# A Winograd-style convolution with batch norm and SiLU: new order of the start-up, and two weight sums on another engine

## The chip, the cores and the metric

The kernel runs on one core of a Trainium2 chip. The metric is device time in microseconds, as the median of several executions; smaller is better. A core has a matrix engine (TensorE, PE in the profile; its weight loads are PEld), a vector engine (VectorE, DVE), an activation engine (ScalarE, ACT), a general engine (GpSimd, POOL) and an engine that here only issues transfers (SyncE, SP). Each engine works through its own list of instructions in the order in which the program issues them; semaphores hold an instruction back until what it reads is there.

## The reference

`x` is bf16 of shape (2, 2048, 1024), `w` is (3, 1024, 1024), and `mean`, `var`, `g`, `b` have 1024 entries each.

```python
def reference(x, w, mean, var, g, b):
    xp = jnp.pad(x, ((0, 0), (1, 1), (0, 0)))
    y = sum(jnp.einsum('bsc,cd->bsd', xp[:, k:k + S, :], w[k]) for k in range(3))
    inv_std = 1.0 / jnp.sqrt(var + 1e-5)
    y = (y - mean) * (g * inv_std) + b
    return _silu(y)
```

So it is a convolution over the sequence with three taps, from 1024 to 1024 channels, then a per-channel scale and shift, then SiLU.

## The kernel before

**The algorithm.** The three-tap convolution is done as F(6, 3): six outputs from eight inputs with eight products instead of eighteen. A sequence of 2048 gives 342 tiles of six outputs. Three steps follow one another.

1. *Input transform* (`transform`, matmuls of L216). A window of up to 128 rows of `x` (21 tiles of six rows, plus two) is the stationary operand, and a small matrix `Rm` of 8 x 21 columns is the moving one. One matmul for each of eight channel blocks turns the window and applies the 8 x 8 transform at once. ScalarE (L230) or Vector (L232) evicts the result from PSUM into `T_sb`, whichever has less in a running count called `load`. There are 17 windows for each of the two batches.
2. *Weight transform.* The output channels are cut into eight chunks of 128. For a chunk the raw taps w0, w1, w2 (tile `wch`) give six transformed taps (tile `uch`, two buffers), in three pairs: a sum of the outer taps, `e` (names e1, e2, eh, fp32), then `e + odd` and `e - odd`, where for pairs 1 and 2 some taps are scaled first (`w0x`, `w1x`, `w2x`). Sums and taps are GpSimd's (L160 to L162); the scalings are ScalarE's (L148), for chunk 0 and part of chunk 1 GpSimd's (L146). Products 0 and 7 use raw taps.
3. *Products and inverse transform* (`unit`). A unit is one chunk and one batch, written (chunk, batch): 16 in all, in the order (0,0), (0,1), (1,0), ... Each has eight products of eight matmuls with 342 columns (L241), in the order 1, 3, 2, 4, 5, 7, 6, 0, into four banks A, B, C, G of PSUM. ScalarE copies partial results (`m1`, `m3`, `s1`, `s2`, `m5`, L280), and Vector combines them to six outputs `y` (L273, L305), the last of which, `y[0]`, needs product 0. ScalarE's SiLU (L317) is issued later, inside the next unit, from the list `late`; a transposing transfer and stores through SyncE bring the unit out.

**The order of the work.** The schedule is the program's order, written by hand. The start transforms batch 0. Inside that loop stand the loads of chunk 0 (L88), the parameter loads and, behind window 5, chunk 0's weight transform on GpSimd. Just before the last window `turn_params` transposes the parameters on PE (L182) and Vector copies them (L183); `make_params` then works out scale and shift on GpSimd. Next comes batch 1's loop: three groups of transforms per window, and between them the matmuls of unit (0,0), which here begins with product 7, in portions given by `want`, so that 52 of its 64 matmuls are spread over 51 groups. The remaining units follow one another.

**Where the weights of later chunks stand.** Ahead of each unit (dc, 1) the program issues the weight transform of chunk dc + 1 on GpSimd and ScalarE, then the unit itself. GpSimd has nothing else to do and runs ahead of PE as far as its buffers and inputs allow.

**Loads.** All x windows and weights go through SyncE's queue in the order of issue; the x windows of 256 KB have rows of 2 KB, chunk loads (256 KB for one tap) have rows of 256 bytes. Ten window buffers are in use. The first window has a buffer of its own, `xw0`, whose row 0 is zeroed. The matrix `Rm` is built from an iota (`val`, GpSimd), a comparison (`E`, Vector) and 25 multiply-adds on Vector (L116) for rows 1 to 6, and by eight selects on GpSimd (L128) for rows 0 and 7.

Of the kernel before, what the change touches and what calls it, by code (L numbers as in the profile page):

```python
# [30 lines left out]
NJ = 8  # L31
# [4 lines left out]
def kernel(  # L36
# [52 lines left out]

    open_weights(0)  # L90

    dummy = consts.tile([P, 2], FP32, name="dummy")
    nc.vector.memset(dummy, 0.0)
    nc.scalar.activation(dummy[:, 1:2], dummy[:, 0:1], ACT.Silu)


    xw0 = consts.tile([P, C], BF16, name="xw0")
    nc.gpsimd.memset(xw0[0:1, :], 0.0)
    Rm = consts.tile([P, NJ, WT], BF16, name="Rm")
    val = consts.tile([P, NJ, WT], I32, name="val")  # L100
    nc.gpsimd.iota(val, pattern=[[-1, NJ], [-M_OUT, WT]], base=0, channel_multiplier=1)
    E = consts.tile([P, NJ, WT], FP32, name="E")
    nc.vector.memset(Rm, 0.0)
    nc.vector.tensor_single_scalar(E, val, 0.0, op=ALU.is_equal)
    for k in range(NJ):
        j = 1
        while j < 7:
            v = BT[j][k]
            if v == 0:
                j += 1  # L110
                continue
            j1 = j
            while j1 + 1 < 7 and BT[j1 + 1][k] == v:
                j1 += 1
            nj = j1 - j + 1
            nc.vector.scalar_tensor_tensor(  # L116
                out=Rm[:, j:j1 + 1, :],
                in0=E[:, k:k + 1, :].to_broadcast([P, nj, WT]) if nj > 1 else E[:, k:k + 1, :],
                scalar=float(v),
                in1=Rm[:, j:j1 + 1, :],  # L120
                op0=ALU.mult,
                op1=ALU.add,
            )
            j = j1 + 1
    for j in (0, 7):
        for k in range(NJ):
            if BT[j][k] != 0:
# [9 lines left out]
    ident = consts.tile([P, P], BF16, name="ident")  # L137
    make_identity(nc, ident)
    yTs = [consts.tile([P, M_OUT, NP], BF16, name=f"yT{i}") for i in range(2)]

    def scale_weights(dc, taps=(2, 1, 0), on_gpsimd=False):
        for k in taps:
# [7 lines left out]
    def open_chunk(dc):  # L150
        wts[dc] = upool.tile([P, 6, CT, P], BF16, name="uch")

    def pair_weights(dc, n):

        w0, w1, w2 = raw[dc]
        e = wtmp.tile([P, CT, P], FP32, name=("e1", "e2", "eh")[n])
        a = wx[dc, 0] if n == 2 else w0
        c = wx[dc, 2] if n == 1 else w2
        odd = wx[dc, 1] if n else w1
        nc.gpsimd.tensor_tensor(e, a, c, op=ALU.add)  # L160
        nc.gpsimd.tensor_tensor(wts[dc][:, 2 * n], e, odd, op=ALU.add)  # L161
        nc.gpsimd.tensor_tensor(wts[dc][:, 2 * n + 1], e, odd, op=ALU.subtract)  # L162

    T_sb = [tpool.tile([P, CT, NJ, NTB], BF16, name=f"T_sb{bi}") for bi in range(B)]
    load = {"act": 0.0, "dve": 1.0}
    EVAC = {"act": (0.17, 0.14), "dve": (0.12, 0.17)}

    prm = consts.tile([4 * DC, P], BF16, name="prm")
    prmT = consts.tile([P, 4, DC], FP32, name="prmT")
    sk = consts.tile([P, DC], FP32, name="sk")  # L170
    beta = consts.tile([P, DC], FP32, name="beta")
    mhalf = consts.tile([P, DC], FP32, name="mhalf")
    rstd = consts.tile([P, DC], FP32, name="rstd")
    sc = consts.tile([P, DC], FP32, name="sc")

    def load_params():
        for q, ap in enumerate((var, g, mean, b)):
            nc.gpsimd.dma_start(out=prm[q * DC:(q + 1) * DC, :], in_=ap.rearrange("(dc p) -> dc p", p=P))

    def turn_params(bk):  # L180
        pv = ps_all[:, bk * 512:bk * 512 + 2 * DC].bitcast(BF16)
        nc.tensor.transpose(pv, prm, ident[0:4 * DC, 0:4 * DC])  # L182
        nc.vector.tensor_copy(prmT.rearrange("p q d -> p (q d)"), pv)  # L183

    def make_params():
        nc.gpsimd.memset(mhalf, -0.5)
        nc.gpsimd.tensor_scalar(rstd, prmT[:, 0, :], 1e-5, 1.0, op0=ALU.add, op1=ALU.mult)
        nc.gpsimd.tensor_tensor(rstd, rstd, mhalf, op=ALU.pow)
        nc.gpsimd.tensor_tensor(sc, prmT[:, 1, :], rstd, op=ALU.mult)
        nc.gpsimd.tensor_tensor(beta, prmT[:, 2, :], sc, op=ALU.mult)  # L190
        nc.gpsimd.tensor_tensor(beta, prmT[:, 3, :], beta, op=ALU.subtract)
        nc.gpsimd.tensor_scalar(sk, sc, C1, 0.0, op0=ALU.mult, op1=ALU.add)

    epool = ctx.enter_context(tc.tile_pool(name="epool", bufs=1))

    def load_window(xpool, bi, wi):
        ntile = min(WT, NTB - WT * wi)
# [53 lines left out]
    def unit(dc, bi, c0, c1, banks, yT, late, pace=(1, 0, 1, 1, 0), seven_first=False):  # L251

        nn = c1 - c0  # L260
        A, B_, C_, G = [ps_all[:, k * 512:k * 512 + nn] for k in banks]
        bA, bB, bC, bG = banks
        pace = list(pace)

        def et(name):
            return epool.tile([P, NTB], FP32, name=name)[:, 0:nn]

        m1, m3, m5, s1, s2, d1 = (et(n) for n in ("m1", "m3", "m5", "s1", "s2", "d1"))
        y_all = epool.tile([P, M_OUT, NTB], FP32, name="y")[:, :, 0:nn]
        y = [y_all[:, i] for i in range(M_OUT)]  # L270

        def stt(o, i0, s, i1, op1=ALU.add):
            nc.vector.scalar_tensor_tensor(out=o, in0=i0, scalar=s, in1=i1, op0=ALU.mult, op1=op1)  # L273
            load["dve"] += 0.0013 * nn

        def copy_out(dst, src):
            for _ in range(pace.pop(0)):
                if late:
                    late.pop(0)()
            nc.scalar.copy(dst, src)  # L280
            load["act"] += 0.0013 * nn

        if seven_first:
            yield from mms(bG, 7, dc, bi, c0, c1, True)
        yield from mms(bA, 1, dc, bi, c0, c1, True)
        copy_out(m1, A)
        yield from mms(bB, 3, dc, bi, c0, c1, True)
        copy_out(m3, B_)
        yield from mms(bA, 2, dc, bi, c0, c1, False)
        copy_out(s1, A)  # L290
        stt(d1, m1, 2.0, A, op1=ALU.subtract)
        yield from mms(bB, 4, dc, bi, c0, c1, False)
        copy_out(s2, B_)
        for i in (2, 4):
            stt(y[i], B_, ALPHA * 2.0 ** i, s1)
        stt(B_, m3, 2.0, B_, op1=ALU.subtract)
        yield from mms(bC, 5, dc, bi, c0, c1, True)
        copy_out(m5, C_)
        while late:
            late.pop(0)()  # L300
        for i in (1, 3, 5):
            stt(y[i], B_, ALPHA * 2.0 ** i, d1)
        if not seven_first:
            yield from mms(bG, 7, dc, bi, c0, c1, True)
        nc.vector.tensor_tensor(y[5], G, y[5], op=ALU.add)  # L305
        yield from mms(bC, 6, dc, bi, c0, c1, False)
        for i in (2, 4):
            stt(y[i], C_, BETA * 0.5 ** i, y[i])
        stt(G, m5, 2.0, C_, op1=ALU.subtract)
        yield from mms(bA, 0, dc, bi, c0, c1, False)  # L310
        for i in (1, 3, 5):
            stt(y[i], G, BETA * 0.5 ** i, y[i])
        stt(y[0], s2, ALPHA, A)
        stt(y[0], C_, BETA, y[0])

        def silu(i0, i1):
            nc.scalar.activation(  # L317
                yT[:, i0:i1:2, c0:c1],
                y_all[:, i0:i1:2],
                ACT.Silu,  # L320
                bias=beta[:, dc:dc + 1],
                scale=sk[:, dc:dc + 1],
            )

        late.extend(lambda i=i: silu(*i) for i in ((2, 5), (1, 6), (0, 1)))
# [10 lines left out]
    with tc.tile_pool(name="xwin", bufs=10) as xpool:  # L336
        for wi in range(NWIN):
            window = load_window(xpool, 0, wi)
            if wi == 1:
                load_chunk(0, 0)  # L340
                load_chunk(0, 2)
                load_params()
            if wi == 2:
                load_chunk(0, 1)
            for h in range(2):
                transform(0, wi, window, 4 * h, 4, (2 * wi + h) % 4 * 2, 2)
            if wi == 5:
                open_chunk(0)
                for n, taps in ((0, ()), (1, (2, 1)), (2, (0,))):
                    scale_weights(0, taps, on_gpsimd=True)  # L350
                    pair_weights(0, n)
            if wi == NWIN - 2:
                turn_params((2 * wi + 2) % 4 * 2)
        make_params()
        for yT in yTs:
            nc.gpsimd.memset(yT[:, :, NTB:NP], 0.0)

        first = unit(0, 0, 0, NTB, (0, 1, 2, 3), yTs[0], late, seven_first=True)
        load["act"] = load["dve"] = 0.0
        gi, done = 0, 0  # L360
        for wi in range(NWIN):
            window = load_window(xpool, 1, wi)
            if wi == 6:
                for k in (0, 2, 1):
                    load_chunk(1, k)
            for ct0, n in ((0, 3), (3, 3), (6, 2)):
                transform(1, wi, window, ct0, n, 4 + gi % 4, 3)
                gi += 1
                want = 52 * gi // (3 * NWIN)
                run(first, want - done)  # L370
                done = want
        load_weights(1)
# [42 lines left out]
    for ui, (dc, bi) in enumerate(units[1:-1], 1):  # L415
        yT = yTs[ui % 2]
        half = 4 * (ui % 2)
        if bi == 1 and dc + 1 < DC:
            open_chunk(dc + 1)
            pair_weights(dc + 1, 0)  # L420
            if dc == 0:
                scale_weights(1, (2,), on_gpsimd=True)
                scale_weights(1, (1, 0))
            else:
                scale_weights(dc + 1)
            for n in (1, 2):
                pair_weights(dc + 1, n)
        run(unit(dc, bi, 0, NTB, (half, half + 1, half + 2, half + 3), yT, late))
        if ui < len(units) - 2:
            late.append(lambda dc=dc, bi=bi, yT=yT: finish(dc, bi, yT))  # L430
# [89 lines left out]
```

## Time and profile before

| | |
|---|---|
| time, three executions | 195.18, 195.74 (median), 196.20 us |
| profiled execution | 196.92 us, of which the span of instructions is 195.1 us |
| PE busy | 177.8 us (91%) |
| POOL busy | 164.7 us (84%) |
| DVE busy | 149.4 us (77%) |
| ACT busy | 124.2 us (64%) |
| mean granted clock of TensorE | 0.979 |
| first transform, first product | 5.40 us, 22.66 us |
| moved by DMA | 31.72 MB, mean 163 GB/s |

The profile is that of one execution. Times in it are counted from the first instruction. A line of a timeline gives start, duration, engine, source line and operation, output and inputs with their shapes, and in brackets the idle time before it and what ended that. A merged line (x40) stands for instructions that followed each other without a pause. The table by stages gives each engine's busy time in a stretch of time, then the granted clock, the share of the DMA engines and the rate in GB/s.

### The profile page before, as it was taken

Reading aid. Unit: us, or ns where it says so; the run is one execution under the profiler, and the core shown is the slowest. Engines: PE = TensorE matmul, PEld = TensorE weight load, DVE = VectorE, ACT = ScalarE, POOL = GpSimd, SP = SyncE. Lnnn points to the kernel's source line nnn. Section 1 sums busy time; section 2 is a strip of 40 time slices with the busy share of each in tenths; the row PEclk is TensorE's granted clock in tenths of the full one; section 3 lists DMA queues with packets and bytes.
Section 4 is the critical chain, followed back from the end, with each engine's and each line's share of the span. In section 5 each row is a group of like instructions: output and inputs, shape, how many; then the busy total and the mean of one; then the engine's idle time right before and its main releaser. Section 6 shows DMA issues by size and latency. Waiting matters only on the chain.

```text
span 195.1 us, 3898 instructions
## 1 busy us (share of the span) xinstructions
PE 177.8 (91%) x1397; PEld 126.7 (65%) x1397; DVE 149.4 (77%) x345; ACT 124.2 (64%) x206; POOL 164.7 (84%) x105
## 2 busy tenths in 40 slices
PE   0779799989999999999999999999999999999840
PEld 0668588856666666666666666666666666679830
DVE  6369668996878696969696969686877878697880
ACT  3479558878378827873786287548736872827930
POOL 7899999999999999999999999999999999800000
PEclk9999879999999999999999999999999999999995
DMA  4999999900607487999292989774755657397505
GB/s 135 277 392 344 332 257 371 284 15 2 116 5 137 96 159 182 276 166 200 39 211 41 198 229 257 142 157 92 139 112 116 129 105 152 76 174 157 115 5 108
DMA packets 86823, 31.72 MB, mean 163 GB/s; under 512 B 73428, under 2 KB 82644, under 8 KB 86804
## 3 DMA queue, kind: packets, MB, share of 16 engines
q1 hardware_dynamic: 86637, 31.46, 69.8%
q8 instruction: 11, 0.18, 0.3%
q14 instruction: 8, 0.07, 0.1%
q0 software_dynamic: 128, 0.01, 0.0%
q10 hardware_dynamic: 39, 0.01, 0.0%
HBM read 14.82 MB, written 8.39 MB: 119 GB/s over the span
## 4 chain that ended last, share of the span: by engine, by line
PE 84%; DVE 7%; DMA 3%; SPq 2%; ACT 1%; issue 1%; DVEq 0%; ACTq 0%
PE ps_all L241 76%; PE ps_all L216 7%; DVE T_sb L232 4%; DMA xw<-in_x_dram 3%; DVE y L273 1%; SPq L206 1%; SPq L88 1%; PE ps_all L446 1%; DVE o_end L478 1%; DVE o_end L486 0%; ACT m L280 0%; ACT yT L317 0%; SPq L203 0%; SPq L202 0%; DVE ps_all L273 0%
## 5 line engine op out<-in xcount | busy, mean ns | idle before, releaser
L241 PE MATMUL ps_all<-T_sb,uch 128*128 128x342 bf16 (+2 forms) x816 | 123.9, 299 | 1.8 <-ACT m L280 1.8
L241 PEld LDWEIGHTS <-uch 128*128 128x128 bf16 x816 | 76.7, 97 | 34.5 <-issue 1.3
L317 ACT ACTIVATE yT<-y,beta,sk 128x684 bf16<-128x684 f32 (+8 forms) x51 | 47.1, 925 | 29.9 <-DVE y L273 29.8
L273 DVE SCALAR_TENSOR_TENSOR y<-ps_all,y 128x342 f32<-128x342 f32 (+2 forms) x102 | 45.4, 487 | 1.3
L241 PE MATMUL ps_all<-T_sb,wch 128*128 128x342 bf16 (+2 forms) x272 | 44.7, 303 | 0.1
L216 PE MATMUL ps_all<-Rm,xw 128*128 128x168 bf16 (+1 forms) x272 | 31.8, 248 | 8.5 <-DVE Rm L116 5.4
L280 ACT COPY m<-ps_all 128x342 f32<-128x342 f32 (+2 forms) x51 | 21.7, 427 | 20.6 <-PE ps_all L241 19.6
L230 ACT CAST T_sb<-ps_all 128x672 bf16<-128x672 f32 (+5 forms) x45 | 26.2, 606 | 13.0 <-PE ps_all L216 12.0
L216 PEld LDWEIGHTS <-xw 128*128 128x128 bf16 (+1 forms) x272 | 24.1, 104 | 14.9 <-POOL ident masks.py:199 5.4
L241 PEld LDWEIGHTS <-wch 128*128 128x128 bf16 x272 | 26.0, 98 | 11.6 <-DVE T_sb L232 0.3
L232 DVE CAST T_sb<-ps_all 128x672 bf16<-128x672 f32 (+3 forms) x40 | 26.1, 698 | 8.4 <-PE ps_all L216 8.2
L273 DVE SCALAR_TENSOR_TENSOR d<-m,ps_all 128x342 f32<-128x342 f32 (+2 forms) x17 | 8.3, 490 | 21.0 <-ACT s L280 21.0
L273 DVE SCALAR_TENSOR_TENSOR y<-ps_all,d 128x342 f32<-128x342 f32 (+2 forms) x51 | 22.0, 486 | 0.6
L273 DVE SCALAR_TENSOR_TENSOR y<-ps_all,s 128x342 f32<-128x342 f32 (+2 forms) x34 | 15.2, 489 | 6.3 <-ACT s L280 6.3
L161 POOL TENSOR_TENSOR uch<-e,w1x 128x1024 bf16<-128x1024 f32 x8 | 17.0, 2131 | 1.2 <-ACT w1x L148 0.7
L160 POOL TENSOR_TENSOR e<-wch 128x1024 f32<-128x1024 bf16 x8 | 17.0, 2125 | 0.8 <-DMA wch<-in_w_dram 0.8
L161 POOL TENSOR_TENSOR uch<-eh,w1x 128x1024 bf16<-128x1024 f32 x8 | 17.0, 2131 | 0.6
L161 POOL TENSOR_TENSOR uch<-e,wch 128x1024 bf16<-128x1024 f32 x8 | 17.0, 2129 | 0.6
L160 POOL TENSOR_TENSOR e<-wch,w2x 128x1024 f32<-128x1024 bf16 x8 | 17.0, 2125 | 0.3 <-ACT w2x L148 0.2
L160 POOL TENSOR_TENSOR eh<-w0x,wch 128x1024 f32<-128x1024 bf16 x8 | 17.0, 2124 | 0.1
L162 POOL TENSOR_TENSOR uch<-e,wch 128x1024 bf16<-128x1024 f32 x8 | 17.1, 2133 | 0.0
L162 POOL TENSOR_TENSOR uch<-eh,w1x 128x1024 bf16<-128x1024 f32 x8 | 17.1, 2132 | 0.0
(46 smaller groups left out, 113.6 us busy)
## 6 DMA issues: line engine op xcount, KB each, us to landing
xw<-in_x_dram SPq DMA_DIRECT2D x30, 256.0 KB
out_dram<-o_sb SPq DMA_DIRECT2D x28, 192.0 KB
wch<-in_w_dram SPq DMA_DIRECT2D x9, 512.0 KB
out_dram<-o_sb SPq DMA_DIRECT2D x14, 120.0 KB
wch<-in_w_dram SPq DMA_DIRECT2D x6, 256.0 KB
xw<-in_x_dram SPq DMA_DIRECT2D x2, 224.0 KB
out_dram<-o_before SPq DMA_DIRECT2D x2, 192.0 KB
o_sb<-yT SPq DMA_TRANSPOSE x14
```

The source lines that it names most:

```text
L88: nc.sync.dma_start(out=raw[dc][k], in_=w_all[:, k, :, dc * P:(dc + 1) * P])
L160: nc.gpsimd.tensor_tensor(e, a, c, op=ALU.add)
L161: nc.gpsimd.tensor_tensor(wts[dc][:, 2 * n], e, odd, op=ALU.add)
L162: nc.gpsimd.tensor_tensor(wts[dc][:, 2 * n + 1], e, odd, op=ALU.subtract)
L206: nc.sync.dma_start(out=xw[0:kk, :], in_=x[bi, t_lo:t_hi + 1, :])
L216: nc.tensor.matmul(banks[:, at:at + NJ * ntile], lhsT=xw[0:kk, (ct0 + c) * P:(ct0 + c + 1) * P], rhs=Rm[0:kk, :, 0:ntile], start=True, sto ...
L230: nc.scalar.copy(dst, src)
L232: nc.vector.tensor_copy(dst, src)
L241: nc.tensor.matmul(ps_all[:, bk * 512:bk * 512 + c1 - c0], lhsT=lhsT, rhs=T_sb[bi][:, ct, j, c0:c1], start=start and ct == 0, stop=ct == C ...
L273: nc.vector.scalar_tensor_tensor(out=o, in0=i0, scalar=s, in1=i1, op0=ALU.mult, op1=op1)
L280: nc.scalar.copy(dst, src)
L317: nc.scalar.activation(yT[:, i0:i1:2, c0:c1], y_all[:, i0:i1:2], ACT.Silu, bias=beta[:, dc:dc + 1], scale=sk[:, dc:dc + 1],)
```

## The change

It has these parts.

- **Matrix.** Rows 1 to 6 of `Rm` are built with 12 multiply-adds from sums that row pairs share (`parts`); only rows 0 and 7 are zeroed first. Row 0 of `xw0` is zeroed by Vector, behind the matrix, not by GpSimd ahead of the iota.
- **Parameters.** They are loaded at the very start through ScalarE's queue, transposed after window 0, and stay in PSUM (`prmT` is a view of bank 0). Vector makes `rstd`'s argument, scale and shift from there; GpSimd only the power. The zeroing of the padding of `yT` moves to the start.
- **Dummy matmuls.** Seven matmuls of 512 columns on a zeroed tile `warm` precede the first transform.
- **Loads.** Chunk 0's taps 0, 2 and 1 are loaded behind windows 3, 5 and 13 (before: behind windows 1, 1 and 2), chunk 1's behind window 10 of batch 1 (before: 6).
- **Chunk 0.** Behind window 7 GpSimd makes the three outer sums with the scalings that they need, and behind window 13 the six taps.
- **Unit (0,0).** Product 0 stands between products 5 and 6 (before: last), and its matmuls begin one group later.
- **Later chunks.** `pair_weights` becomes `pair_sum` and `pair_tap`, in the same order; for chunks 3 and 5 the first sum is issued on Vector.

```diff
+    prm = consts.tile([4 * DC, P], BF16, name="prm")
+    for q, ap in enumerate((var, g, mean, b)):
+        nc.scalar.dma_start(out=prm[q * DC:(q + 1) * DC, :], in_=ap.rearrange("(dc p) -> dc p", p=P))
...
-    xw0 = consts.tile([P, C], BF16, name="xw0")
-    nc.gpsimd.memset(xw0[0:1, :], 0.0)
...
+    parts = consts.tile([P, 3, 2, WT], FP32, name="parts")
+    warm = consts.tile([P, 512], BF16, name="warm")
+    nc.vector.memset(warm, 0.0)
+    nc.vector.memset(Rm[:, 0:NJ:NJ - 1, :], 0.0)
     nc.vector.tensor_single_scalar(E, val, 0.0, op=ALU.is_equal)
-    for k in range(NJ):
-        j = 1
-        while j < 7:
...
+    for n, odd in enumerate((1.0, 2.0, 0.5)):
+        row = BT[2 * n + 1]
+        rstt(parts[:, n], E[:, 1:3], row[2], E[:, 5:7])
+        rstt(parts[:, n], E[:, 3:5], row[4], parts[:, n])
+        rstt(Rm[:, 2 * n + 1], parts[:, n, 0], odd, parts[:, n, 1])
+        rstt(Rm[:, 2 * n + 2], parts[:, n, 0], -odd, parts[:, n, 1])
+    nc.vector.memset(xw0[0:1, :], 0.0)
...
+    for yT in yTs:
+        nc.gpsimd.memset(yT[:, :, NTB:NP], 0.0)
...
+    def pair_sum(dc, n, engine=nc.gpsimd):
+        e = outer[dc, n] = wtmp.tile([P, CT, P], FP32, name=("e1", "e2", "eh")[n])
+        a = wx[dc, 0] if n == 2 else raw[dc][0]
+        c = wx[dc, 2] if n == 1 else raw[dc][2]
+        engine.tensor_tensor(e, a, c, op=ALU.add)
+
+    def pair_tap(dc, n, op):
+        odd = wx[dc, 1] if n else raw[dc][1]
+        nc.gpsimd.tensor_tensor(wts[dc][:, 2 * n + (op == ALU.subtract)], outer[dc, n], odd, op=op)
...
+    prmT = ps_all[:, 512 - 2 * DC:512].bitcast(BF16).rearrange("p (q d) -> p q d", q=4)
+
+    def turn_params():
+        nc.tensor.transpose(prmT.rearrange("p q d -> p (q d)"), prm, ident[0:4 * DC, 0:4 * DC])
+        nc.vector.tensor_scalar(rstd, prmT[:, 0, :], 1e-5, 1.0, op0=ALU.add, op1=ALU.mult)
+        nc.gpsimd.tensor_tensor(rstd, rstd, mhalf, op=ALU.pow)
...
+    for _ in range(7):
+        nc.tensor.matmul(ps_all[:, 7 * 512:8 * 512], lhsT=warm[:, 0:P], rhs=warm, start=True, stop=True)
...
-        if not seven_first:
-            yield from mms(bG, 7, dc, bi, c0, c1, True)
+        yield from mms(*((bA, 0) if seven_first else (bG, 7)), dc, bi, c0, c1, not seven_first)
...
-        yield from mms(bA, 0, dc, bi, c0, c1, False)
+        if not seven_first:
+            yield from mms(bA, 0, dc, bi, c0, c1, False)
...
-            if wi == 1:
-                load_chunk(0, 0)
-                load_chunk(0, 2)
-                load_params()
-            if wi == 2:
-                load_chunk(0, 1)
+            if wi in (3, 5, 13):
+                load_chunk(0, {3: 0, 5: 2, 13: 1}[wi])
...
+            if wi == 0:
+                turn_params()
-            if wi == 5:
+            if wi == 7:
                 open_chunk(0)
-                for n, taps in ((0, ()), (1, (2, 1)), (2, (0,))):
+                for n, taps in ((0, ()), (1, (2,)), (2, (0,))):
                     scale_weights(0, taps, on_gpsimd=True)
-                    pair_weights(0, n)
-            if wi == NWIN - 2:
-                turn_params((2 * wi + 2) % 4 * 2)
+                    pair_sum(0, n)
+            if wi == 13:
+                pair_tap(0, 0, ALU.add)
+                scale_weights(0, (1,), on_gpsimd=True)
+                for n, op in ((1, ALU.add), (0, ALU.subtract), (1, ALU.subtract), (2, ALU.add), (2, ALU.subtract)):
+                    pair_tap(0, n, op)
...
-            if wi == 6:
+            if wi == 10:
                 for k in (0, 2, 1):
                     load_chunk(1, k)
...
-                want = 52 * gi // (3 * NWIN)
+                want = 52 * max(gi - 1, 0) // (3 * NWIN - 1)
...
-            for n in (1, 2):
-                pair_weights(dc + 1, n)
+            for n in range(0 if dc else 1, 3):
+                pair_sum(dc + 1, n, nc.vector if n == 0 and dc in (2, 4) else nc.gpsimd)
+                for op in (ALU.add, ALU.subtract):
+                    pair_tap(dc + 1, n, op)
         run(unit(dc, bi, 0, NTB, (half, half + 1, half + 2, half + 3), yT, late))
```

More of the change, by code (lines that the diff above doesn't have):

```diff
@@ L101, with rstt @@
     nc.gpsimd.iota(val, pattern=[[-1, NJ], [-M_OUT, WT]], base=0, channel_multiplier=1)
+    xw0 = consts.tile([P, C], BF16, name="xw0")
     E = consts.tile([P, NJ, WT], FP32, name="E")
-    nc.vector.memset(Rm, 0.0)
+    parts = consts.tile([P, 3, 2, WT], FP32, name="parts")
+    warm = consts.tile([P, 512], BF16, name="warm")
+    nc.vector.memset(warm, 0.0)
+    nc.vector.memset(Rm[:, 0:NJ:NJ - 1, :], 0.0)
     nc.vector.tensor_single_scalar(E, val, 0.0, op=ALU.is_equal)
-    for k in range(NJ):
-        j = 1
-        while j < 7:
[L108 to L124, printed above, removed]
+    def rstt(o, i0, f, i1):
+        nc.vector.scalar_tensor_tensor(out=o, in0=i0, scalar=float(f), in1=i1, op0=ALU.mult, op1=ALU.add)
+    for n, odd in enumerate((1.0, 2.0, 0.5)):
+        row = BT[2 * n + 1]
+        assert [odd * row[k + 1] for k in (1, 3, 5)] == row[1:6:2] and row[6] == 1
+        rstt(parts[:, n], E[:, 1:3], row[2], E[:, 5:7])
[3 more added lines that the diff above has]
+    nc.vector.memset(xw0[0:1, :], 0.0)
     for j in (0, 7):
@@ L151, in open_chunk @@
         wts[dc] = upool.tile([P, 6, CT, P], BF16, name="uch")
[L153 to L162, printed above, removed]
+    outer = {}
+    def pair_sum(dc, n, engine=nc.gpsimd):
[6 more added lines that the diff above has]
+        nc.gpsimd.tensor_tensor(wts[dc][:, 2 * n + (op == ALU.subtract)], outer[dc, n], odd, op=op)
     T_sb = [tpool.tile([P, CT, NJ, NTB], BF16, name=f"T_sb{bi}") for bi in range(B)]
@@ L166 @@
     EVAC = {"act": (0.17, 0.14), "dve": (0.12, 0.17)}
-    prm = consts.tile([4 * DC, P], BF16, name="prm")
-    prmT = consts.tile([P, 4, DC], FP32, name="prmT")
     sk = consts.tile([P, DC], FP32, name="sk")
@@ L174 @@
     sc = consts.tile([P, DC], FP32, name="sc")
[L176 to L183, printed above, removed]
-    def make_params():
[L186 to L192, printed above, removed]
+    prmT = ps_all[:, 512 - 2 * DC:512].bitcast(BF16).rearrange("p (q d) -> p q d", q=4)
[3 more added lines that the diff above has]
+        nc.gpsimd.tensor_tensor(rstd, rstd, mhalf, op=ALU.pow)
+    def make_params():
+        nc.vector.tensor_tensor(sc, prmT[:, 1, :], rstd, op=ALU.mult)
+        nc.vector.tensor_tensor(beta, prmT[:, 2, :], sc, op=ALU.mult)
+        nc.vector.tensor_tensor(beta, prmT[:, 3, :], beta, op=ALU.subtract)
+        nc.vector.scalar_tensor_tensor(out=sk, in0=prmT[:, 1, :], scalar=C1, in1=rstd, op0=ALU.mult, op1=ALU.mult)
+    nc.gpsimd.memset(mhalf, -0.5)
     epool = ctx.enter_context(tc.tile_pool(name="epool", bufs=1))
+    for _ in range(7):
+        nc.tensor.matmul(ps_all[:, 7 * 512:8 * 512], lhsT=warm[:, 0:P], rhs=warm, start=True, stop=True)
     def load_window(xpool, bi, wi):
@@ L338 @@
             window = load_window(xpool, 0, wi)
-            if wi == 1:
-                load_chunk(0, 0)
-                load_chunk(0, 2)
-                load_params()
-            if wi == 2:
-                load_chunk(0, 1)
+            if wi in (3, 5, 13):
+                load_chunk(0, {3: 0, 5: 2, 13: 1}[wi])
             for h in range(2):
                 transform(0, wi, window, 4 * h, 4, (2 * wi + h) % 4 * 2, 2)
-            if wi == 5:
+            if wi == 0:
+                turn_params()
+            if wi == 7:
                 open_chunk(0)
-                for n, taps in ((0, ()), (1, (2, 1)), (2, (0,))):
+                for n, taps in ((0, ()), (1, (2,)), (2, (0,))):
                     scale_weights(0, taps, on_gpsimd=True)
-                    pair_weights(0, n)
-            if wi == NWIN - 2:
-                turn_params((2 * wi + 2) % 4 * 2)
+                    pair_sum(0, n)
[4 more added lines that the diff above has]
+                    pair_tap(0, n, op)
         make_params()
-        for yT in yTs:
-            nc.gpsimd.memset(yT[:, :, NTB:NP], 0.0)
         first = unit(0, 0, 0, NTB, (0, 1, 2, 3), yTs[0], late, seven_first=True)
@@ L419 @@
             open_chunk(dc + 1)
-            pair_weights(dc + 1, 0)
             if dc == 0:
+                pair_sum(1, 0)
+                for op in (ALU.add, ALU.subtract):
+                    pair_tap(1, 0, op)
                 scale_weights(1, (2,), on_gpsimd=True)
@@ L425 @@
                 scale_weights(dc + 1)
-            for n in (1, 2):
-                pair_weights(dc + 1, n)
+            for n in range(0 if dc else 1, 3):
+                pair_sum(dc + 1, n, nc.vector if n == 0 and dc in (2, 4) else nc.gpsimd)
+                for op in (ALU.add, ALU.subtract):
+                    pair_tap(dc + 1, n, op)
         run(unit(dc, bi, 0, NTB, (half, half + 1, half + 2, half + 3), yT, late))
```

## The prediction

> **What bounds the kernel now.** I read the page first (engine shares, the chain that ended last), then the waits, then the timelines of single engines at the places that the diff touches.
>
> ```profile
> PE 177.8 (91%) x1397; PEld 126.7 (65%) x1397; DVE 149.4 (77%) x345; ACT 124.2 (64%) x206; POOL 164.7 (84%) x105
> PE 84%; DVE 7%; DMA 3%; SPq 2%; ACT 1%; issue 1%; DVEq 0%; ACTq 0%
> ```
>
> The chain is TensorE for 84% of the span. In order of time it shows SyncE issues and x transfers until 10.9 us, transforms and evictions of batch 0 until 22.66, then PE almost without a break until 183. So what is gained before 22.66, or as a PE gap up to 42, reaches the end, and so does every new PE gap later. The start, from PE's timeline:
>
> ```profile
> 20.59 0.18 PE L182 MATMUL ps_all<-ident,prm 32*128 32x32 bf16 x1
> 21.83 0.70 PE L216 MATMUL ps_all<-Rm,xw 33*128 33x48 bf16 x11 [1.06 <-DVE prmT L183]
> 22.66 0.32 PE L241 MATMUL ps_all<-T_sb,wch 128*128 128x342 bf16 x1
> ```
>
> The parameter transpose makes PE wait 1.06 us for Vector's copy; product 7 of unit (0,0) (chunk 0, batch 0) begins at 22.66. By stages, the clock then fell:
>
> ```profile
> 23.28:26.67 3.39, 3.39 (x22) 2.72 (x20) 1.88 (x3) 1.42 (x3) 3.23 (x3) 0.50 1.08 219
> ```
>
> The first number after the stage is its length, then come the engines' busy times, the granted clock (0.50), the DMA share and GB/s. From unit (1,0) on, a product takes 1.16 us and a unit 9.29. GpSimd makes one weight chunk per two units. Its timeline for chunk 3:
>
> ```profile
> 74.17 2.13 POOL L160 TENSOR_TENSOR e<-wch 128x1024 f32<-128x1024 bf16 x1
> 76.38 2.13 POOL L161 TENSOR_TENSOR uch<-e,wch 128x1024 bf16<-128x1024 f32 x1
> 78.47 2.14 POOL L162 TENSOR_TENSOR uch<-e,wch 128x1024 bf16<-128x1024 f32 x1
> 80.56 2.13 POOL L160 TENSOR_TENSOR e<-wch,w2x 128x1024 f32<-128x1024 bf16 x1
> 82.77 2.13 POOL L161 TENSOR_TENSOR uch<-e,w1x 128x1024 bf16<-128x1024 f32 x1
> 84.85 2.13 POOL L162 TENSOR_TENSOR uch<-e,w1x 128x1024 bf16<-128x1024 f32 x1
> 86.94 2.13 POOL L160 TENSOR_TENSOR eh<-w0x,wch 128x1024 f32<-128x1024 bf16 x1
> 89.15 2.13 POOL L161 TENSOR_TENSOR uch<-eh,w1x 128x1024 bf16<-128x1024 f32 x1
> 91.24 2.14 POOL L162 TENSOR_TENSOR uch<-eh,w1x 128x1024 bf16<-128x1024 f32 x1
> ```
>
> These are sum e1, taps 1 and 2, sum e2, taps 3 and 4, sum eh, taps 5 and 6. A chunk takes 19.16 us (74.17 to chunk 4's e1 at 93.33), two units of PE 18.58. So GpSimd is nearly as loaded as PE; it only began early. PE and Vector nearby:
>
> ```profile
> 81.72 5.97 PE L241 MATMUL ps_all<-T_sb,uch 128*128 128x342 bf16 x40
> 91.00 5.97 PE L241 MATMUL ps_all<-T_sb,uch 128*128 128x342 bf16 x40
> 84.34 0.51 DVE L273 SCALAR_TENSOR_TENSOR y<-ps_all,y 128x342 f32<-128x342 f32 x1
> 86.25 0.51 DVE L273 SCALAR_TENSOR_TENSOR d<-m,ps_all 128x342 f32<-128x342 f32 x1 [1.39 <-ACT s L280]
> ```
>
> Unit (2,1) starts at 81.72, unit (3,0), the first user of chunk 3, at 91.00, in the order 1, 3, 2, 4, 5, 7, 6, 0. Product 5 starts at 91.00 + 4 x 1.16 = 95.64; tap 5 was ready at 91.28, so GpSimd has 4.36 us to spare there. In chunk 7 only 2.05 are left (165.78 + 2.13 against 165.30 + 4.64). Vector finishes unit (2,0) (its last `y[0]`) at 84.85, 3.13 us inside unit (2,1).
>
> **Start: matrix, dummies, parameters.** Rm now takes 12 Vector instructions instead of 25 (2.91 us, 0.116 apart): 1.4 to 1.7 us. The iota moves from 1.73 to about 0.75 as the `xw0` memset leaves GpSimd (0.94 there; on Vector I keep 0.94 as its price, the upper bound, and it stands last before the first matmul). Seven 512-column dummies at the 0.15 us that the first 168-column matmuls took (16 in 2.40) are about 0.45 each, 3.2 in all, from about 1.6. First transform about 4.8 instead of 5.40. Parameters on ScalarE's queue: four issues at GpSimd's 0.52 to 0.76 put the table load (1.28 us) at about 2.9 and its end near 4.2, before the first eviction. Their landing after 3.9 to 4.4 us (by GpSimd's queue) would be at 5 to 7 us; transpose, `rstd` and whatever Vector and PE queue behind them wait until then, up to 1.5 us. The pause before window 6 (next part) takes that up; no cost, at most 0.5. The four parameter operations that go to Vector, at GpSimd's 0.20 each, stand where product 7 begins; Vector waited 0.70 for PE there (23.30), which covers nearly all of the 0.8.
>
> **Loads.** The DMA rates by microsecond add up to 5.05 MB, all x of batch 0 and chunk 0, at 17.6 us. The change only reorders these transfers: windows 0 to 3 come unhindered, and pauses stand before windows 6 and 14. The last window lands about 1 us behind its bytes (window 2: bytes 7.3, matmul 8.29), near 18.7; its transforms and last two evictions (0.36 to 0.86 each) give product 7 at about 20.4. The evictions, 0.78 us a window, end by then too, as the 1.06 us parameter wait is gone. Gain 2.25 us; bounds 1.1 (that wait alone) and 2.8.
>
> **Chunk 0 on GpSimd.** Outer taps land at about 10.9 (2.1 MB by 10.0). Three sums and two scalings, 3 x 2.13 + 2 x 1.04 = 8.5: 19.4. Tap 1's load is in by 17, then six taps and one scaling, 13.8: tap 1 at 21.5, tap 3 at 24.7, then 2.1 apart to tap 6 at 33.1. PE asks for them from 23.3 on, one product per 2.67 us, product 6 at 38. Never late, 1.3 us or more to spare. The parameter arithmetic (30.21 to 33.3) and the yT memsets leave this place, so chunk 1 begins at 33.1 instead of 33.83.
>
> **Unit (0,0).** Product 0 between 5 and 6 covers the wait of product 6 for ScalarE's copy of `m5` (0.71 us at 41.69): gain 0.7, bounds 0 and 0.8. The products of this unit also start one group of transforms later, as `want` counts from the second; the work is the same, so nothing. Loading chunk 1 behind window 10: window 11 lands at 30.2 to 31.4 and is due at 20.4 + 11 x 1.02 = 31.6; no cost, at most 0.5.
>
> **The clock.** Half speed over 3.39 us cost 1.70. The new start has pauses too, before windows 6 and 14; even odds, 0.85. Start in all: 2.25 + 0.7 + 0.85 = 3.8 earlier, bounds 2.0 and 4.9.
>
> **Sums e1 of chunks 3 and 5 on Vector.** This decides. It takes 2.1 us off GpSimd, but the instruction is issued where unit (2,1) begins, so Vector has it behind `y[0]` of unit (2,0). Call the start of (2,1) U. Vector is free at U + 3.13. Price: 342, 245 and 97 columns take 0.510, 0.409 and 0.253, that is 0.151 + 1.049 per thousand, so 1.23 for 1,024 (bounds 0.7 from the 768-column copy's 0.558, and GpSimd's 2.13). It fits in the 1.39 us in which Vector waits for ScalarE, so `d1` behind it is not delayed. It ends at U + 4.40. GpSimd, at chunk 3 by about U - 5 (0.7 us earlier than before, and without its 0.65 us wait in chunk 1, against a U that is 3.8 earlier), stands at tap 1 and everything behind it waits. From the e1 end, by the rows above: tap 3 after 8.52 (84.90 - 76.38), tap 4 10.60, tap 5 14.90, tap 6 17.00. PE reaches product 3 at U + 9.29 + 1.16 = 10.45, tap 3 is there at 12.92: 2.47 us lost. Product 4 is then not late (15.24 against 15.00). Product 5 would start at 16.40, its tap comes at 19.30: 2.90 lost. Product 6: 21.62 against 21.40. Loss 5.37 in unit (3,0), whatever the start gained, as U moves along.
>
> GpSimd has then no lead left: chunk 4's tap 5 comes 21.40 + 17.11 = 38.51 after U, PE wants it at 9.29 + 18.58 + 5.37 + 4.64 = 37.88; with the 0.04 that e1 starts ahead, 0.6 more. Chunk 5 repeats 5.37. Chunks 6 and 7 lose 19.16 - 18.58 = 0.58 each. Sum 10.74 + 3 x 0.58 = 12.5.
>
> **Clock after these waits.** At 23.28 the clock fell behind a gap of 1.06 us and shorter ones. A fall behind the 2.47 gap is swallowed by the 2.90 one; a fall behind the second costs up to 1.70 per chunk. I put in 0.2 each, 0.4.
>
> The Trainium skill, page "TensorE: Matmul & The Clock Gate", section "Why this matters for your kernels", lets the clock fall only behind idle gaps above about 3 us between bursts. The row at 23.28 speaks against it: the longest gap before it was 1.06. By the page the two stalls would keep full clock, and the estimate would be 0.4 lower.
>
> **Sum.** 12.5 - 3.8 + 0.4 = 9.1 us slower. The profiled execution took 196.92 (span 195.1 plus 1.8 around it) and would become 206.0; it lies 1.2 over the median 195.74, so I predict 204.8.
>
> **Rivals.** *Faster:* Vector's sum comes in time and GpSimd keeps its lead. For it: Vector sits 21.0 us waiting for ScalarE's `s`, and chunk 3's weights landed long before. Against: Vector works in program order, as ScalarE's scalings show (issued at the same place, run behind the previous unit's `m5`). It decides at U - 0.97: an e1 that ends before that costs nothing. Then the start's 3.8 stand alone: 191.9. Chance 0.10. *No difference:* only one of the two sums is late and the start brings its upper bound, 5.4 - 4.9: 196.2. Chance 0.03. *Clock:* both chunks end in half clock, 204.4 + 2 x 1.70 = 207.8. Chance 0.15. *Start without gain:* PE begins product 7 hardly earlier, as windows 6 and 14 come late (2.0 instead of 3.8): 206.6. Chance 0.10. My forecast has 0.62.
>
> **Range.** With e1 at 0.7 (1.1 less) and a start of 4.9 the slow case gives 202.2 without clock falls; with e1 at 2.13 (1.8 more) and a start of 2.0 it gives 208.4. 201.5 to 208.0 leaves out the two cases on the other side and little more. This kernel's times can tell 0.5%, 1 us, from no change. Slower 0.87, same 0.03, faster 0.10.
>
> **What will show it.** GpSimd's first taps of chunks 3 and 5 wait some 9 and 7 us for Vector's `e`; PE waits for GpSimd's `uch` twice in each of units (3,0) and (5,0), near 2.5 and 2.9 us; product 7 of (0,0) starts near 20.4 and PE's wait for `m5` is gone. Wrong if GpSimd runs on without that wait, or if PE shows no idle time after 60 us.

## The result: 5% slower

The changed kernel takes 205.98 us (median of 4 executions, 205.82 to 208.07) against 195.92 of the kernel before; the ratio is 1.054, 95% interval 1.047 to 1.062. The profiled execution took 206.11 us, with a span of 204.3.

The page of the changed kernel: busy times, then the chain that ended last by engine and by line.

```profile
PE 182.4 (89%) x1404; PEld 126.7 (62%) x1404; DVE 152.2 (75%) x340; ACT 124.4 (61%) x206; POOL 156.3 (76%) x93
...
POOL 37%; PE 36%; DMA 8%; DVE 8%; issue 5%; ACT 2%; SPq 1%; POOLq 1%; DVEq 0%; ACTq 0%
PE ps_all L242 31%; POOL uch L165 24%; POOL e L161 8%; DMA xw<-in_x_dram 8%; POOL eh L161 5%; PE ps_all L217 5%; DVE y L274 4%; DVE T_sb L233 1%; POOLq L518 1%; ACT yT L318 1%; SPq L207 1%; DVE ps_all L274 1%; DVE e L161 1%; ACT m L281 1%; DVE o_end L481 0%
```

GpSimd is busy 8 us less, and yet it now carries 37% of the chain, where PE had 84%. The waits (who waited for whom: us in all, times, longest) say why:

```profile
POOL uch L165 <- DVE e L161: 16.6, 2, 10.0
...
PE ps_all L242 <- POOL uch L165: 9.3, 7, 2.7
```

Two waits of GpSimd for Vector's sums turn into seven waits of PE for taps; neither line exists before. The timelines of Vector, GpSimd and PE around chunk 3, whose unit (2,1) begins at 78.82 (that is U):

```profile
81.45 0.52 DVE L274 SCALAR_TENSOR_TENSOR y<-ps_all,y 128x342 f32<-128x342 f32 x1
81.88 1.22 DVE L161 TENSOR_TENSOR e<-wch 128x1024 f32<-128x1024 bf16 x1
83.35 0.51 DVE L274 SCALAR_TENSOR_TENSOR d<-m,ps_all 128x342 f32<-128x342 f32 x1 [0.26 <-ACT s L281]
```

```profile
83.24 4.22 POOL L165 TENSOR_TENSOR uch<-e,wch 128x1024 bf16<-128x1024 f32 x2 [9.95 <-DVE e L161]
```

```profile
88.11 1.33 PE L242 MATMUL ps_all<-T_sb,uch 128*128 128x342 bf16 x8
91.80 3.65 PE L242 MATMUL ps_all<-T_sb,uch 128*128 128x342 bf16 x24 [2.37 <-POOL uch L165]
98.17 1.34 PE L242 MATMUL ps_all<-T_sb,uch 128*128 128x342 bf16 x8 [2.72 <-POOL uch L165]
...
102.82 5.98 PE L242 MATMUL ps_all<-T_sb,uch 128*128 128x342 bf16 x40
```

Vector's sum runs right behind `y[0]`, GpSimd stands 9.95 us, and in unit (3,0) PE waits before products 3 and 5. Unit (3,0) begins at 88.11 and unit (3,1) at 102.82: 14.71 instead of 9.29, 5.42 lost. From the unit starts in the same way (112.12 to 121.97, 131.26 to 145.60, 154.90 to 164.78, 174.08 to 183.95): 0.56 in chunk 4, 5.05 in 5, 0.59 in 6, 0.58 in 7. In all 12.20 lost.

The start gave 2.90, the distance of U from 81.72. 12.20 - 2.90 = 9.3; the spans differ by 204.3 - 195.1 = 9.2. The sums of the waits are smaller than the loss (9.3 of 12.20), because a wait is counted only from the modelled end of the last matmul and because the clock fell once (next section but one).

### The profile page after: what moved, and what is told of

Read it like the earlier page. It is cut to its first block, busy times and chain, and to the rows that moved or that the text cites. A ratio compares the mean times of both kernels' runs of the same rounds, so it can differ in the third digit from the quotient of the medians.

```text
span 204.3 us, 3897 instructions
## 1 busy us (share of the span) xinstructions
PE 182.4 (89%) x1404; PEld 126.7 (62%) x1404; DVE 152.2 (75%) x340; ACT 124.4 (61%) x206; POOL 156.3 (76%) x93
## 4 chain that ended last, share of the span: by engine, by line
POOL 37%; PE 36%; DMA 8%; DVE 8%; issue 5%; ACT 2%; SPq 1%; POOLq 1%; DVEq 0%; ACTq 0%
PE ps_all L242 31%; POOL uch L165 24%; POOL e L161 8%; DMA xw<-in_x_dram 8%; POOL eh L161 5%; PE ps_all L217 5%; DVE y L274 4%; DVE T_sb L233 1%; POOLq L518 1%; ACT yT L318 1%; SPq L207 1%; DVE ps_all L274 1%; DVE e L161 1%; ACT m L281 1%; DVE o_end L481 0%
## 5 line engine op out<-in xcount | busy, mean ns | idle before, releaser
L242 PE MATMUL ps_all<-T_sb,uch 128*128 128x342 bf16 (+2 forms) x816 | 126.3, 302 | 10.4 <-POOL uch L165 9.3
L242 PE MATMUL ps_all<-T_sb,wch 128*128 128x342 bf16 (+2 forms) x272 | 44.1, 300 | 0.1
L165 POOL TENSOR_TENSOR uch<-e,w1x 128x1024 bf16<-128x1024 f32 x16 | 33.8, 2133 | 0.6
L217 PE MATMUL ps_all<-Rm,xw 128*128 128x168 bf16 (+1 forms) x272 | 30.6, 245 | 3.0 <-DMA xw<-in_x_dram 2.5
L231 ACT CAST T_sb<-ps_all 128x672 bf16<-128x672 f32 (+5 forms) x45 | 26.3, 606 | 8.3 <-PE ps_all L217 7.1
L274 DVE SCALAR_TENSOR_TENSOR ps_all<-m,ps_all 128x342 f32<-128x342 f32 (+2 forms) x34 | 16.6, 488 | 0.0
L161 POOL TENSOR_TENSOR e<-wch 128x1024 f32<-128x1024 bf16 x6 | 12.8, 2126 | 3.2 <-DMA wch<-in_w_dram 3.2
L281 ACT COPY s<-ps_all 128x342 f32<-128x342 f32 (+2 forms) x34 | 14.3, 421 | 0.4 <-PE ps_all L242 0.2
```

The source lines that it names most:

```text
L161: engine.tensor_tensor(e, a, c, op=ALU.add)
L165: nc.gpsimd.tensor_tensor(wts[dc][:, 2 * n + (op == ALU.subtract)], outer[dc, n], odd, op=op)
L217: nc.tensor.matmul(banks[:, at:at + NJ * ntile], lhsT=xw[0:kk, (ct0 + c) * P:(ct0 + c + 1) * P], rhs=Rm[0:kk, :, 0:ntile], start=True, sto ...
L242: nc.tensor.matmul(ps_all[:, bk * 512:bk * 512 + c1 - c0], lhsT=lhsT, rhs=T_sb[bi][:, ct, j, c0:c1], start=start and ct == 0, stop=ct == C ...
```

## The experiments

The theory: Vector's place in its own program makes the two sums late, and GpSimd's lead is gone. The rivals: GpSimd is too slow for an earlier PE whoever sums; a sum on Vector costs by itself; the loss needs the new start.

**All first sums on GpSimd** (`gp_sums`).

```diff
-                pair_sum(dc + 1, n, nc.vector if n == 0 and dc in (2, 4) else nc.gpsimd)
+                pair_sum(dc + 1, n)
```

> The changed kernel with all first sums on GpSimd again. Theory (the two sums stand behind y[0] on Vector, and GpSimd loses its lead while it waits for them): both long waits of GpSimd and PE's waits of 5.4, 0.6, 5.1, 0.6 and 0.6 us in units (3,0) to (7,0) go, only some 0.2 us at chunk 7 may stay, since PE is now 2.9 us earlier against GpSimd's 0.7: about 193.2 us. Rival (GpSimd's pace of 19.16 us per chunk is too slow for a PE that starts earlier, whoever makes the sums): waits of PE in every chunk, 200 us or more.

194.25 us; ratio to the kernel before 0.989 (0.982 to 0.996). That is 1.1 above the 193.2 expected, but the kernel before, measured beside it, was 1.1 above its earlier median too (196.98 for 195.92). The rest of the change is a small gain, and one expression costs some 12 us: 11.7 by the medians, 12.8 by the two ratios. Of all PE waits for GpSimd this one is left, in chunk 7, as expected:

```profile
166.88 1.34 PE L242 MATMUL ps_all<-T_sb,uch 128*128 128x342 bf16 x8 [0.23 <-POOL uch L165]
```

**The same sums on Vector, one unit earlier** (`early_sum`).

```diff
+        if bi == 0 and dc in (2, 4):
+            pair_sum(dc + 1, 0, nc.vector)
         if bi == 1 and dc + 1 < DC:
...
-                pair_sum(dc + 1, n, nc.vector if n == 0 and dc in (2, 4) else nc.gpsimd)
+                if n or dc not in (2, 4):
+                    pair_sum(dc + 1, n)
```

> The changed kernel with the two sums on Vector still, but issued one unit earlier, ahead of units (2,0) and (4,0). Theory: Vector ends the sum of chunk 3 at 69.5 + 4.4 = 73.9 us, GpSimd reaches chunk 3 at 73.2, so it waits under 1 us and then has 2.1 us less to do; PE does not wait: about 193.0 us. Rival (a sum on Vector costs by itself, by delaying Vector's d1 or by slowing GpSimd's operations beside it): 1 us or more above the kernel with all sums on GpSimd.

193.91 us, ratio 0.987 (0.980 to 0.994). Same operations, same engines, another place: 12.1 us less than the changed kernel, by the medians. Not Vector as such but the sum's place in Vector's program is the cost. GpSimd's two waits are now short, though a little over the 1 us expected:

```profile
74.11 4.23 POOL L165 TENSOR_TENSOR uch<-e,wch 128x1024 bf16<-128x1024 f32 x2 [1.23 <-DVE e L161]
...
111.52 4.23 POOL L165 TENSOR_TENSOR uch<-e,wch 128x1024 bf16<-128x1024 f32 x2 [1.23 <-DVE e L161]
```

The rival's cost by itself does not show in the time, but something of it does in Vector's row (last section).

**The kernel before with the two sums on Vector, nothing else** (`before_dve`).

```diff
-            pair_weights(dc + 1, 0)
+            pair_weights(dc + 1, 0, nc.vector if dc in (2, 4) else nc.gpsimd)
```

> The kernel before with nothing changed but the first sums of chunks 3 and 5 on Vector. Theory: the loss hangs on Vector's place relative to unit (2,1), not on the new start: 5.4 + 0.6 + 5.2 + 0.6 + 0.6 = 12.4 us more, about 208.3. Rival (the loss needs the earlier PE of the new start): under 200.

208.69 us beside 196.98 of the kernel before: 11.7 more by the medians, ratio 1.063 (1.050 to 1.076). By the starts of the units its profile loses 5.43, 0.56, 5.05, 0.58 and 0.58 us in chunks 3 to 7, 12.20 in all, as the changed kernel does. The loss does not need the new start. PE's waits in chunk 3 are those of the changed kernel:

```profile
93.29 3.65 PE L241 MATMUL ps_all<-T_sb,uch 128*128 128x342 bf16 x24 [2.37 <-POOL uch L161]
99.66 1.34 PE L241 MATMUL ps_all<-T_sb,uch 128*128 128x342 bf16 x8 [2.72 <-POOL uch L161]
```

**Chunk 3's sum alone on Vector** (`only_chunk3`).

```diff
-                pair_sum(dc + 1, n, nc.vector if n == 0 and dc in (2, 4) else nc.gpsimd)
+                pair_sum(dc + 1, n, nc.vector if n == 0 and dc == 2 else nc.gpsimd)
```

> The changed kernel with chunk 3's first sum alone on Vector. Theory: 5.4 us in unit (3,0), and then no lead is left, so each of chunks 4 to 7 costs 19.16 - 18.58 = 0.58 more: 5.4 + 4 x 0.58 = 7.7 over the kernel with all sums on GpSimd, about 200.8. Rival (each sum on Vector is a cost by itself and nothing follows): half of the total, about 199.3.

202.34 us, 8.1 over `gp_sums` (7.7 expected, 6 by the rival). So one late sum also costs in every chunk that follows; PE's timeline has the wait in product 5 of chunks 4 to 7:

```profile
117.45 1.33 PE L242 MATMUL ps_all<-T_sb,uch 128*128 128x342 bf16 x8 [0.40 <-POOL uch L165]
136.59 1.34 PE L242 MATMUL ps_all<-T_sb,uch 128*128 128x342 bf16 x8 [0.38 <-POOL uch L165]
155.76 1.34 PE L242 MATMUL ps_all<-T_sb,uch 128*128 128x342 bf16 x8 [0.42 <-POOL uch L165]
174.92 1.34 PE L242 MATMUL ps_all<-T_sb,uch 128*128 128x342 bf16 x8 [0.41 <-POOL uch L165]
```

**Each of Vector's sums twice** (`twice_sum`).

```diff
-        engine.tensor_tensor(e, a, c, op=ALU.add)
+        for _ in range(2 if engine is nc.vector else 1):
+            engine.tensor_tensor(e, a, c, op=ALU.add)
```

> The changed kernel with each of Vector's two sums issued twice (the second writes the same values). Theory: the sum ends 1.22 us later in the unit, GpSimd's taps come 1.22 later, PE's loss is about 6.6 in unit (3,0) and 6.3 in unit (5,0), the 0.6 per later chunk stays: 2.4 us above the changed kernel, about 208.4. Vector's d1 is then 1.1 us late, which its slack in the unit takes up. Rival (PE waits for something that this sum does not time): as the changed kernel, 206.

208.34 us, 2.4 over the changed kernel by the medians, as computed; the ratios to the kernel before, 1.064 (1.058 to 1.070) and 1.054 (1.047 to 1.062), differ by less and their intervals overlap. The profile is clearer:

```profile
88.04 1.33 PE L243 MATMUL ps_all<-T_sb,uch 128*128 128x342 bf16 x8
92.98 7.70 PE L243 MATMUL ps_all<-T_sb,uch 128*128 128x342 bf16 x32 [3.62 <-POOL uch L166]
...
104.00 5.98 PE L243 MATMUL ps_all<-T_sb,uch 128*128 128x342 bf16 x40
```

Unit (3,0) lasts 15.96, so 6.67 are lost, 1.25 more than in the changed kernel; in unit (5,0) it is 6.34, 1.29 more. The second sum adds 1.25 to the first (2.47 for both). What Vector's sum takes goes into the loss one to one.

**Without the dummy matmuls** (`early_nodummy`, like the next ones on top of `early_sum`): `range(7)` becomes `range(0)`.

> The kernel with the two sums issued one unit earlier, without the seven dummy matmuls. Theory (the start is set by the landing of windows 4, 6 and 14, so a slower PE before window 4 costs nothing): 193.9 us, within 0.5. Rival (the dummies keep the clock up until the products begin): half clock for some 3.4 us at the start, 0.5 to 1.7 us more.

194.12 us (12 executions): no difference to `early_sum`'s 193.91 or 193.95 that this measurement shows. What the dummies do can be seen in the profile: the 24 matmuls of windows 1 to 3 take 3.54 us without them and 2.19 with them (`early_sum`), that is 0.15 and 0.09 each. The time does not show it; PE then waits 0.21 us for window 4 instead of 0.70. `early_nodummy`, then `early_sum`:

```profile
5.93 3.54 PE L217 MATMUL ps_all<-Rm,xw 128*128 128x168 bf16 x24
9.68 1.54 PE L217 MATMUL ps_all<-Rm,xw 128*128 128x168 bf16 x16 [0.21 <-DMA xw<-in_x_dram]
```

```profile
5.98 2.19 PE L217 MATMUL ps_all<-Rm,xw 128*128 128x168 bf16 x24
8.88 1.55 PE L217 MATMUL ps_all<-Rm,xw 128*128 128x168 bf16 x16 [0.70 <-DMA xw<-in_x_dram]
```

**Product 0 last again** (`early_zero_last`): the two lines of `unit` as before.

> The kernel with the two sums issued one unit earlier, with product 0 of unit (0,0) last again. Theory: PE waits again 0.7 us for ScalarE's copy of m5 between products 5 and 6: 194.6 us. Rival (another order of the evictions has taken that wait away already): 193.9.

194.87 us, 0.9 more than `early_sum`. The expected wait is back in PE's timeline; the times alone, with ratios of 0.993 (0.990 to 0.996) and 0.990 (0.986 to 0.994, `early_sum_again`), would not carry it.

```profile
39.43 0.31 PE L242 MATMUL ps_all<-T_sb,uch 128*128 128x342 bf16 x1 [0.71 <-ACT m L281]
```

**Tap 1 of chunk 0 behind the last window** (`late_tap`): the load and the six taps move from window 13 to the last window.

> The kernel with the two sums issued one unit earlier, with chunk 0's tap 1 loaded behind the last x window of batch 0 instead of behind window 13. Theory (the DMA queue sets the start: 0.26 MB in rows of 256 bytes stand ahead of windows 14 to 16): product 7 of unit (0,0) begins 0.8 to 1.3 us earlier, and GpSimd, busy with the outer sums until 20.0 us, loses nothing: about 192.9 us. Rival (the evictions set the start): no difference; or tap 1 lands so late that PE waits for chunk 0's taps: slower.

194.31 us: no gain. The expectation failed. In this profile the clock is half from 13.4 to 16.8 us, the transforms run without a pause from 12.54 on, and product 7 begins at 22.55; whether the load order would have helped at full clock stays open.

**Once more, beside the next two** (`early_sum_again`).

> The kernel with the two sums issued one unit earlier, once more with more rounds, beside the next two. 193.9 us, 1.2% below the kernel before.

193.95 us, ratio 0.990 (0.986 to 0.994). It can't be told from `gp_sums` (194.25, 0.989), so the sums on Vector bring nothing measurable even where they come early.

**Small dummies in the pauses** (`early_warm`):

```diff
             if wi == 0:
                 turn_params()
+            for _ in range({3: 10, 5: 10, 13: 8}.get(wi, 0)):
+                nc.tensor.matmul(ps_all[:, 512 + 424:2 * 512], lhsT=warm[:, 0:P], rhs=warm[:, 0:88], start=True, stop=True)
```

> The same with 10, 10 and 8 small dummy matmuls (88 columns) behind windows 3, 5 and 13, where PE waits about 1 us for the next window. Theory (half clock at 12 to 17 us, seen in some profiles, comes from these pauses and costs about 0.6 us in those executions): no half clock before the products, 0.2 to 0.6 us below early_sum in the median, less spread. Rival (the pauses do not set the clock, or the landing of the windows alone sets the start): no difference, or 0.3 more where the dummies delay a window.

194.90 us, 0.9 above `early_sum_again`, with a ratio of 0.994 (0.990 to 0.998). The gain did not come; the spread (193.67 to 196.64, against 193.20 to 196.84) hardly shrank. The profile, of the slowest of the twelve executions, has no half clock at 12 to 17 us, but one from 19.5 to 26.3, around a wait of 2.46 us for window 14. What keeps the clock up in the start is not settled.

**Chunk 0's loads at their old places** (`early_oldload`): taps 0, 2 and 1 behind windows 1, 1 and 2, sums behind window 5.

> The same, with chunk 0's taps loaded behind windows 1, 1 and 2 as in the kernel before, and its weight sums behind window 5. Theory (only the order of the loads changes, and with the parameter wait gone the evictions end at about 21.6 us): product 7 begins within 0.4 us of where it did (21.2 to 22.2), 193.5 to 194.5 us. Rival (the new order of the loads is what brings the gain of the start): 1 us or more slower, 195 us.

194.68 us, 0.7 above `early_sum_again`, between the two expectations; the intervals overlap (0.994, 0.991 to 0.998). Inconclusive in the time. But the order of the loads seems to bear on the clock: the mean granted clock was 0.971 to 0.974 in nine of the twelve executions here, and in two of twelve in `early_sum_again` (0.972 and 0.974, the others 0.979 to 0.995). In this profile it was half from 9.3 to 16.1 us, and product 7 began at 23.58, outside the 21.2 to 22.2 expected.

## Why the prediction was right

**The deciding step held in its parts.** Price of the sum: 1.23 predicted, 1.22 measured. Place: free at U + 3.13, started at U + 3.06. GpSimd's first tap: U + 4.40, came at U + 4.42. Loss in (3,0): 5.37, measured 5.42. Chunks 4, 6 and 7: 0.6, 0.58 and 0.58, measured 0.56, 0.59 and 0.58. All losses: 12.5, measured 12.20. `before_dve`, `early_sum` and `twice_sum` show that place and duration of this instruction make the loss, and `only_chunk3` that the lost lead costs on.

**Chunk 5 was a little less,** 5.05 for 5.37. There Vector began the sum at 124.65, 2.68 after unit (4,1)'s start at 121.97: PE's wait in unit (4,0) had let Vector catch up. The prediction took Vector's lag as fixed.

**That the total fits so well is partly luck.** 12.5 - 3.8 + 0.4 = 9.1 stands against 12.20 - 2.90 = 9.3: the start was put 0.9 too high, and the losses (0.3) and the clock after the waits (0.4) were put too high as well, which makes up for most of it.

**The start was mis-sized:** 3.8 predicted, 2.90 measured. Its terms were 2.25 for product 7, 0.7 for `m5` and 0.85 for the clock at 23.28; measured, 0.51, 0.7 and the whole 1.70 give the 2.90. The term that failed is the first, product 7 at 20.4: it came at 22.15. One part is the clock, from the stages of the changed kernel:

```profile
11.92:15.33 3.41, 3.41 (x26) 3.41 (x27) 1.72 (x2) 1.86 (x3) 3.26 (x3) 0.51 1.05 365
23.28:26.67 3.39, 3.39 (x39) 2.87 (x37) 3.01 (x6) 2.85 (x5) 3.39 (x2) 1.00 1.06 375
```

The half clock came behind the pauses before windows 4 and 6, in the transforms. From 15.48 on Vector's evictions then ran without a pause until 22.10, and product 7, which reads all of batch 0's `T_sb`, began 0.05 later:

```profile
15.48 6.62 DVE L233 CAST T_sb<-ps_all 128x672 bf16<-128x672 f32 x9 [0.26 <-PE ps_all L217]
```

```profile
22.15 0.32 PE L242 MATMUL ps_all<-T_sb,wch 128*128 128x342 bf16 x1
```

In `early_sum`'s profile the half clock did not come, and product 7 began at 21.18, still 0.8 later than predicted. There the windows landed late, and Vector's last evictions (from 19.94, 1.12 us) ended at 21.06 instead of 20.4:

```profile
18.12 0.76 PE L217 MATMUL ps_all<-Rm,xw 128*128 128x168 bf16 x8 [0.70 <-DMA xw<-in_x_dram]
19.15 1.07 PE L217 MATMUL ps_all<-Rm,xw 128*128 128x168 bf16 x16 [0.27 <-DMA xw<-in_x_dram]
...
20.75 0.59 PE L217 MATMUL ps_all<-Rm,xw 128*128 128x168 bf16 x6 [0.53 <-DMA xw<-in_x_dram]
21.18 0.31 PE L242 MATMUL ps_all<-T_sb,wch 128*128 128x342 bf16 x1
```

PE waited 0.70 us for window 14 and 0.27 for window 15; the prediction had the last window landed near 18.7. That `want` counts from the second group, so that two groups of batch 1 stand ahead of product 7, was put at nothing and is worth hardly more: in these two profiles product 7 begins 0.05 and 0.12 us behind Vector's last eviction of batch 0, for which it had to wait in any order.

**The clock term was right in the profile for the wrong reason.** I counted half of the 1.70 of the half clock at 23.28 as the change's gain. `before_dve` has the old start, and its profile shows no half clock there: unit (2,1) begins at 80.30 instead of 81.72, although product 7 began 0.23 later (22.89).

```profile
80.30 5.97 PE L241 MATMUL ps_all<-T_sb,uch 128*128 128x342 bf16 x40
```

So that half clock comes in some executions of this start and not in others. It may also be most of the 1.2 us by which the profiled execution lay over its median, which I subtracted at the end; that was not tested. The changed kernel's profiled execution lies only 0.13 over its own median. In executions the difference is 206.11 - 196.92 = 9.2 (9.1 predicted); in medians it is 10.1.

**The `m5` wait** is gone, and `early_zero_last` brings it back with 0.71 us, about the 0.7 it was put at; the times agree with that, but would not show it alone.

**Clock after the long waits.** It fell once, in unit (5,0), behind a gap of 2.00 us:

```profile
134.59 5.33 PE L242 MATMUL ps_all<-T_sb,uch 128*128 128x342 bf16 x24 [2.00 <-POOL uch L165]
140.95 1.34 PE L242 MATMUL ps_all<-T_sb,uch 128*128 128x342 bf16 x8 [1.03 <-POOL uch L165]
```

The 24 matmuls took 5.33 instead of 3.65, and the next wait is 1.03 instead of 2.72: swallowed, as argued, so the 0.4 was not needed. The clock of these 3.24 us:

```profile
134.86:138.10 3.24, 3.24 (x13) 1.70 (x12) 0.00 (x0) 1.05 (x2) 3.24 (x2) 0.50 0.00 0
```

The Trainium skill, page "TensorE: Matmul & The Clock Gate", section "Why this matters for your kernels", asks, against such falls, for no idle gaps above about 3 us between bursts. Here it fell behind 2.00, and in `before_dve` behind 1.98; the measurement decides against that threshold. But in unit (3,0) of both kernels it stayed full behind a gap of 2.37 (24 matmuls in 3.65), so the length of the gap alone does not decide. What does stays open.

**The rivals.** "Vector's sum comes in time" is what `early_sum` makes true: it gives 193.9, 2.0 above the 191.9 of that rival, which took the start's 3.8 us as given. "Start without gain" came true in its condition, product 7 hardly earlier, beside the main mechanism: its 206.6 lies nearer to the median of 205.98 than the forecast's 204.8. Between the two profiled executions, without the 1.2 us subtracted at the end, the forecast is the nearer one: 206.0 for 206.11, and that rival 207.8. "No difference" was priced too low: one late sum costs the later chunks too, by the prediction's own 0.58 a chunk, and `only_chunk3` lost 8.1 for the 5.4 put in.

**Two sums do not come out.** The upper bound of the start, 4.9, is not the sum of its bounds (2.8 + 0.8 + 0.85 = 4.45, or 5.3 with the whole 1.70), and what is left in chunk 7 is 2.03, not 2.05. Neither moves the forecast; the lower corner of the range would be 202.7 or 201.8 instead of 202.2.

## What to carry to other kernels

Work moved to a less busy engine arrives when that engine's program reaches it. Before counting the time saved, find the instruction ahead of it there, and compare its end with the moment when the old engine would have done the job. An engine that starts ahead of the bound but is no faster does not win a lost lead back: GpSimd needs 19.16 us a chunk and PE 18.58, and one late sum cost 5.4 us at once and 0.6 in every later chunk.

## What the hardware showed that was not expected

Vector's sum took 1.22 us while GpSimd stood still (changed kernel), but 2.05 and 2.31 us beside GpSimd's running taps in `early_sum`:

```profile
71.92 2.05 DVE L161 TENSOR_TENSOR e<-wch 128x1024 f32<-128x1024 bf16 x1
...
109.06 2.31 DVE L161 TENSOR_TENSOR e<-wch 128x1024 f32<-128x1024 bf16 x1
```

```profile
68.67 4.22 POOL L165 TENSOR_TENSOR uch<-eh,w1x 128x1024 bf16<-128x1024 f32 x2
...
106.08 4.22 POOL L165 TENSOR_TENSOR uch<-eh,w1x 128x1024 bf16<-128x1024 f32 x2
```

GpSimd's taps end at 72.89 and 110.30, so the sums overlapped them for 0.97 and 1.24 us and became 0.83 and 1.09 longer, while GpSimd's operations kept their length. Vector nearly stood still beside GpSimd, and GpSimd then waited 1.23 us both times, about the length of the sum by itself. So of the 2.13 us that a sum takes off GpSimd, only some 0.9 are left. That the sums bring nothing even when issued early does not need this reason, though: with all sums on GpSimd, PE waits for GpSimd only 0.23 us in all (`gp_sums`), so there was hardly anything to gain. The Trainium skill, page "GPSIMD Engine Reference", section "Specifications", says that the two engines share the SBUF interfaces and contend where a Vector instruction has two SBUF inputs; these rows agree. In both of them GpSimd's tap was running when the sum began and Vector was the one held up; no run shows the opposite order.
